# Seven half products for one more gate-side group of a fused S5 and SwiGLU block, placed beside an output pair

## The chip, the cores and the metric

The kernel runs on one core of one Trainium2 chip. The metric is device time in microseconds (us): 201.05 us is the median of three timed runs of the kernel before (200.91, 201.05 and 201.06). TensorE (PE in the profile) multiplies matrices, VectorE (DVE) and ScalarE (ACT) work elementwise, GpSimd (POOL) here mostly issues accumulating transfers, and SyncE (SP) issues loads and stores. Each engine takes its own instructions in the order in which the program gives them, and waits for the others by semaphores.

## The reference, cut to what matters

```python
xn = layernorm(x)                                # x: 1 x 2048 x 512, bf16
Bu = einsum("bld,pd->blp", xn, B_bar)            # complex, 512 states
h_t = Lam_bar * h_(t-1) + Bu_t                   # over 2048 tokens
y  = 2 * real(einsum("blp,dp->bld", h, C)) + xn * Dskip
glu = (silu(xn @ w1) * (xn @ w3)) @ w2           # 512 -> 1792 -> 512
out = x + y + glu
```

## The kernel before, in words

The 2048 tokens are worked in four blocks of 512 (`b` = 0 to 3). In a block the normalised input lies transposed in `xnT` (four tiles of 128 input features by 512 tokens). `glu` makes 14 tiles of 128 hidden features: gate side `xn @ w1` through Silu into a tile `g16`, up side `xn @ w3` into `u16`, and VectorE multiplies the two into `act`. `bu` makes the inputs of the scan. `ssm_tasks` holds VectorE's share of the state part: `pre_a`, `pre_b` and `pre_c` rotate `Bu` (`pre_c`, L491 to L495, is the last add of the rotation, on VectorE or as an accumulating transfer from GpSimd's queue), four scans per half of the states (L505), and `post_a`, `post_b`, `post_c` rotate the states back into `act`.

The outputs are made in eight pairs of 128-token chunks, `pairs[n]` with n = 0 to 7; pairs 4 and 5 belong to block 2, pairs 6 and 7 to block 3. `y_fast(n)` makes one pair by seven half products (Winograd's form of Strassen's method) of 11 matmuls each, called `product1` to `product7`, in the order 1, 4, 2, 6, 5, 7, 3; for n = 4 and 5 product 3 is put off into the next pair. VectorE prepares each pair with three row sums (`row_sums`, L992 to L1008, two or three on VectorE, the rest as a transfer) and a fourth, `s4` (L1091 to L1096). `seeds(n)` copies residual values into PSUM (the banks that TensorE writes) before the pair's products add to them.

The same seven-product form is used for the up side of block 3 in `glu_last`. The up side's first 12 tiles are three groups of four (`NG` = 3, n = 0 to 2). A group's seven products are here called one, five, two, six, seven, three and last, in the order in which they run. Each is four matmuls with 256 moving columns (`product`, L866 to L872). Product five needs the weight sum `s1`, six needs `s2`, seven `s3`, and three needs `s4`. `up_sums` (L826 to L836) makes `s1` to `s3` for all three groups on VectorE ahead of `glu_last`; `s4` is made per group (L909, L910). ScalarE copies partial results between PSUM banks (L857), and VectorE adds the shared sum `s5` to two results per group (L879). The gate side of all tiles is plain: `gate_side` (L859, `side` at L845 to L851) is four matmuls with 512 moving columns per tile. In each group the four gate tiles stand between the products. `gate` (L862 to L864) multiplies gate and up.

The order of VectorE's work is set by `Filler` (`bg`, L23 to L60). Background work is a queue of tasks with costs; `fill` records tasks while a running estimate of VectorE's time is not more than a lead of 1.7 us past a running estimate of TensorE's. `own` counts work that TensorE's results need at once. `flush(key)` records everything in the queue up to the last task with that key, whatever stands before it.

At the end of the program (L1238 to L1252) pair 3 is followed by `glu_last(3)`, and that by pairs 4 to 7.

Of the kernel before, what the change touches and what calls it, by code (L numbers as in the profile page):

```python
# [17 lines left out]
P = 128  # L18
# [45 lines left out]
def kernel(  # L64
# [397 lines left out]
    def ssm_tasks(b, posts_last=False, between=(), middle=(), late=()):  # L462
# [5 lines left out]
        def half(hf):  # L468
            psl = slice(2 * hf, 2 * hf + 2)
            st = {}  # L470

            def pre_a():
                if b == 0:
                    sin_step((2 * hf + 1, 1))
                    nc.vector.tensor_scalar(out=tabe[:, psl, 2, :], in0=tabe[:, psl, 1, :], scalar1=-1.0,
                                            scalar2=None, op0=ALU.mult)
                st["g"] = u_blk[b, hf]
                if (b, hf) == (3, 0):
                    st["p"] = up.tile(FULL, BF16, name="u")
                elif b == NBLK - 1:  # L480
                    st["p"] = xtp.tile([P, NDT, TBLK], BF16, name="xnT").rearrange("p (j r) t -> p j r t", r=2)
                else:
                    st["p"] = ssmw.tile(FULL, BF16, name="p")
                nc.vector.tensor_tensor(out=st["p"][:, :, ::-1, :], in0=st["g"], in1=tabe[:, psl, 2:0:-1, :],
                                        op=ALU.mult)

            def pre_b():
                nc.vector.tensor_tensor(out=st["g"], in0=st["g"], in1=tabe[:, psl, 0:1, :].to_broadcast(FULL),  # L488
                                        op=ALU.mult)

            def pre_c():  # L491
                if b == 0 or (b, hf) == (2, 0):
                    nc.vector.tensor_tensor(out=st["g"], in0=st["g"], in1=st["p"], op=ALU.add)
                else:
                    gp.dma_start(out=st["g"], in_=st["p"], accum_op=ALU.add)  # L495

            def scan(j, ri):
                pt = 2 * hf + j
                init = 0.0
                if b in (1, 2):  # L500
                    init = ends[:, hf, 2 * j + ri:2 * j + ri + 1]
                elif b > 2:
                    init = act_blk[b - 1][:, CPB - 1, k_state(pt, ri), P - 1:P]
                v = st["g"][:, j, ri, :]
                nc.vector.tensor_tensor_scan(out=v, data0=rho[:, pt:pt + 1].to_broadcast([P, TBLK]), data1=v,  # L505
                                             initial=init, op0=ALU.mult, op1=ALU.add)

            def post_a(csl=slice(0, CPB)):
                if "p16" not in st:
                    st["p16"] = ssmw.tile(FULL, BF16, name="p").bitcast(FP16).rearrange(  # L510
                        "p j r (c t) -> p (j r c t)", t=P).rearrange("p (c k t) -> p c k t", c=CPB, t=P)
                tsl = slice(csl.start * P, csl.stop * P)
                nc.vector.tensor_tensor(out=by_state(st["p16"][:, csl]), in0=by_chunk(st["g"][:, :, ::-1, tsl]),  # L513
                                        in1=by_chunk(tabe[:, psl, 2:0:-1, tsl]), op=ALU.mult)

            def post_b(csl=slice(0, CPB)):
                tsl = slice(csl.start * P, csl.stop * P)
                n = csl.stop - csl.start
                nc.vector.tensor_tensor(out=by_state(act_state(b, hf)[:, csl]), in0=by_chunk(st["g"][:, :, :, tsl]),  # L519
                                        in1=by_chunk(tabe[:, psl, 0:1, tsl]).to_broadcast([P, 2, 2, n, P]), op=ALU.mult)  # L520

            def post_c(csl=slice(0, CPB)):
                a, p16 = act_state(b, hf)[:, csl], st["p16"][:, csl]
                if b == NBLK - 1 and (hf == 1 or csl.start > 0):
                    nc.vector.tensor_tensor(out=a, in0=a, in1=p16, op=ALU.add)
                else:
                    gp.dma_start(out=a, in_=p16, accum_op=ALU.add)  # L527

            if (b, hf) == (1, 1):
                pre_c.ready = lambda: ("squares", 2, CPB - 1) in sins_done  # L530
            pre_a.ready = lambda: (b, hf) in u_blk
            scans = [lambda j=j, ri=ri: scan(j, ri) for j in range(2) for ri in range(2)]
            return (pre_a, pre_b, pre_c), scans, (post_a, post_b, post_c)

        (pre0, scans0, post0), (pre1, scans1, post1) = (half(hf) for hf in range(NPT // 2))

        transfers = (post0[2],) + (() if b == NBLK - 1 else (post1[2],)) + ((pre1[2],) if b > 0 else ()) + ((pre0[2],) if b in (1, 3) else ())

        def add(*fns):
            for fn in fns:  # L540
# [285 lines left out]
    def up_sums(b):  # L826
# [8 lines left out]
                for out, x, z, op in ((s1, a21, a22, ALU.add), (s3, a11, a21, ALU.subtract),  # L835
                                      (s2, s1, a11, ALU.subtract))]  # L836

    def glu_last(b):
        xnT = xnT_blk[b]
        s1, s2, s3, s4 = ups["s"]  # L840
# [33 lines left out]
        def halves(ps):  # L874
            return ps.rearrange("p (h t) -> p h t", h=2)

        def add(out, ps):
            bg.own(0.7)
            nc.vector.tensor_tensor(out=out, in0=halves(ps), in1=halves(s5), op=ALU.add)  # L879

        gates = []
        for f in range(4 * NG, NFT):
# [6 lines left out]
                gates.pop()()  # L889
            if f % 2 == 1:  # L890
                gates.append(lambda f=f, tiles=tiles: gate(f - 1, tiles))
        for n in range(NG):
            f0 = 4 * n
            a11, a12, a22, s1n, s2n, s3n, s4n = (v[:, :, n, :] for v in (
                up_quarter(0, 0), up_quarter(1, 0), up_quarter(1, 1), s1, s2, s3, s4))
            g, e = (ps_y.tile([P, TBLK], FP32, name="y_ps") for _ in range(2))
            f, z = (ps_bu.tile([P, TBLK], FP32, name="bu_ps") for _ in range(2))
            upper, lower = pair_tiles(), pair_tiles()
            product(g, a11, b11, True)
            copy(f, g)  # L900
            product(e, s1n, t1, True)
            copy(s5, e)
            gate_side(f0, upper[0])
            bg.fill(0.8)
            gates.pop()()
            product(f, a12, b21, False)
            product(g, s2n, t2, False)
            copy(e, g)
            bg.own(0.42)  # L909
            nc.vector.tensor_tensor(out=s4n, in0=a12, in1=s2n, op=ALU.subtract)  # L910
            copy(upper[1][:, :, 0:TH], halves(f))
            gate_side(f0 + 1, upper[0])
            bg.fill()
            product(g, s3n, t3, False)
            copy(z, g)
            add(lower[1][:, :, TH:TBLK], g)
            product(e, s4n, b22, False)
            add(upper[1][:, :, TH:TBLK], e)
            gate_side(f0 + 2, lower[0])
            bg.fill()  # L920
            gate(f0, upper)
            product(z, a22, t4, False)
            copy(lower[1][:, :, 0:TH], halves(z))
            gate_side(f0 + 3, lower[0])
            bg.fill()
            gates.append(lambda f0=f0, lower=lower: gate(f0 + 2, lower))
        seeds(4)
        return gates.pop()


    def res_list(b):
# [104 lines left out]
    def y_fast(n, then=(), between=()):  # L1036
# [50 lines left out]
        def product2():  # L1087
            if b == 0:
                bg.first(list(then))
            mms(f, v["a12"], weight(1, D1), False)  # L1090
            v["s4"] = v["a12"]  # L1091
            if n in (2, 3, 4, 5):
                gp.dma_start(out=v["s4"], in_=v["s2"], accum_op=ALU.add)
            else:
                bg.own(0.85, -1.1)
                nc.vector.tensor_tensor(out=v["s4"], in0=v["a12"], in1=v["s2"], op=ALU.add)  # L1096
            add(o1[:, D1], f, o1[:, D1])
            if last:
                store(c1, o1, D1)
            if n + 1 < len(pairs) and n not in (1, 2, 3) and n - 1 not in LATER:  # L1100
                seeds(n + 1)
            steps()

# [43 lines left out]
        for i in ((1, 5, 2, 6, 4, 3, 7) if b == 0 else (1, 2, 4, 6, 5, 7, 3) if b == 1 else ORDER.get(n, (1, 4, 2, 6, 5, 7, 3))):  # L1147
            if i == 3 and n in LATER:
                later[n] = product3
            else:  # L1150
                products[i - 1]()
            if i == 5 and n - 1 in later:
                later.pop(n - 1)()
                if n + 1 < len(pairs):
                    seeds(n + 1)
            if n in LATER:
                bg.fill()
            if between:
                for step in between.popleft():
                    step()  # L1160
                    bg.fill()
                if n == 3 and not between:
                    bg.first(up_sums(3))
            if n == 2 and i == 7:
                seeds(3)

    ln_alloc(0)
    ln1a, ln1b = ln_tasks_vector(1)
# [70 lines left out]
    y_done.append(2)  # L1239
    y_fast(3, (), bu_fast(3, 1))  # L1240
    bg.flush("up")
    gate = glu_last(3)
    gate()
    for n in range(4, len(pairs)):
        ahead = row_sums(n + 1, *pairs[n + 1]) if n + 1 < len(pairs) else ()
        if n > 4:
# [2 lines left out]
        if n == 5:  # L1249
            for t in (difference(3), *last_posts):  # L1250
                bg.add(*t)
        y_fast(n, ahead if n == 4 else ())  # L1252


# [28 lines left out]
```

## Time and profile before

| what | value |
|---|---|
| median of the timed runs | 201.05 us (200.91 to 201.06) |
| span of the profiled execution, first to last instruction | 199.5 us |
| TensorE busy | 195.6 us, 1401 matmuls |
| VectorE busy | 181.8 us, 254 instructions |
| ScalarE busy | 135.0 us, 281 instructions |
| GpSimd busy | 51.5 us, 75 instructions |
| mean granted TensorE clock | 0.999 |
| matmuls of `glu_last` | L848, 64 of them: 15.9 us; L869, 84 of them in groups of 24 and 12 |

No time of the profiled execution other than its span is listed beside the three timed runs. The 1.5 us between the span and the median lie around the first and the last instruction.

The profile page lists busy time per engine, the chain of work that ended last, groups of instructions by source line, and transfers. A timeline lists one engine's instructions in order: start and length in us, line, operation, tiles written and read, and in brackets the idle time just before it with what ended it. Consecutive instructions of one kind are merged (x2 is two). A matmul's listed length contains about 0.16 us of drain beyond its share of the pace, so the step from one start to the next is what it costs in a row. On VectorE too the next instruction often starts some 0.08 us before the listed end of the one before.

### The profile page before, as it was taken

Reading aid. Unit: us, or ns where it says so; the run is one execution under the profiler, and the core shown is the slowest. Engines: PE = TensorE matmul, PEld = TensorE weight load, DVE = VectorE, ACT = ScalarE, POOL = GpSimd, SP = SyncE. Lnnn points to the kernel's source line nnn. Section 1 sums busy time; section 2 is a strip of 40 time slices with the busy share of each in tenths; the row PEclk is TensorE's granted clock in tenths of the full one; section 3 lists DMA queues with packets and bytes.
Section 4 is the critical chain, followed back from the end, with each engine's and each line's share of the span. In section 5 each row is a group of like instructions: output and inputs, shape, how many; then the busy total and the mean of one; then the engine's idle time right before and its main releaser. Section 6 shows DMA issues by size and latency. Waiting matters only on the chain.

```text
span 199.5 us, 3700 instructions
## 1 busy us (share of the span) xinstructions
PE 195.6 (98%) x1401; PEld 130.7 (65%) x1401; DVE 181.8 (91%) x254; ACT 135.0 (68%) x281; POOL 51.5 (26%) x75
## 2 busy tenths in 40 slices
PE   8999999999999999999999999999999999999994
PEld 2774444444444488866555468888566678888893
DVE  3689699999999999989999997999999999999972
ACT  4699897699999996968998684362588783111220
POOL 7180289700411134041202305040021303310000
PEclk9999999999999999999999999999999999999999
DMA  4999996991497054730997455838137732941111
GB/s 138 326 277 200 302 186 124 343 273 23 69 181 141 0 105 82 135 105 0 156 148 119 89 92 98 172 83 132 53 59 129 149 56 52 174 92 36 53 44 40
DMA packets 32258, 25.12 MB, mean 126 GB/s; under 512 B 16240, under 2 KB 29936, under 8 KB 32240
## 3 DMA queue, kind: packets, MB, share of 16 engines
q0 software_dynamic: 6128, 11.38, 33.5%
q1 hardware_dynamic: 25536, 13.21, 26.8%
q10 hardware_dynamic: 576, 0.30, 0.5%
q8 instruction: 11, 0.18, 0.4%
q14 instruction: 7, 0.06, 0.1%
HBM read 7.74 MB, written 2.10 MB: 49 GB/s over the span
## 4 chain that ended last, share of the span: by engine, by line
PE 95%; DMA 2%; SPq 1%; issue 0%; DVE 0%
PE gu_ps L587 34%; PE gu_ps L1054 17%; PE y_ps L1054 10%; PE gu_ps L848 7%; PE bu_ps L1054 7%; PE bu_ps L454 3%; PE y_ps L454 3%; PE y_ps L869 3%; PE y_ps L780 3%; DMA w_sb<-in_B_w_dram 2%; PE gu_ps L619 2%; PE gu_ps L780 2%; PE bu_ps L869 1%; PE bu_ps L780 1%; PE bu_ps L619 1%; SPq L166 0%
## 5 line engine op out<-in xcount | busy, mean ns | idle before, releaser
L587 PE MATMUL gu_ps<-xnT,w_sb 128*128 128x512 bf16 x312 | 69.6, 379 | 0.0
L587 PEld LDWEIGHTS <-w_sb 128*128 128x128 bf16 x312 | 30.5, 98 | 34.2
L1054 PEld LDWEIGHTS <-act 128*128 128x128 f16 x462 | 43.5, 98 | 5.4
L596 ACT ACTIVATE g<-gu_ps 128x512 bf16<-128x512 f32 x41 | 24.8, 606 | 6.0 <-PE gu_ps L587 3.6
L597 ACT ACTIVATE u<-gu_ps 128x512 bf16<-128x512 f32 x41 | 24.8, 606 | 4.5 <-PE gu_ps L587 3.7
L505 DVE TENSOR_TENSOR_SCAN u<-rho,ends,u 128x512 bf16<-128x512 f32 x16 | 20.0, 1270 | 0.0
L527 POOL DMA_DIRECT2D act<-p x7 | 9.2, 1320 | 34.0 <-DVE act L519 22.1
L1054 PE MATMUL gu_ps<-w_sb,act 128*128 128x256 bf16 (+3 forms) x126 | 16.0, 267 | 0.0
L848 PE MATMUL gu_ps<-xnT,w_sb 128*128 128x512 bf16 x64 | 15.9, 379 | 0.0
L604 DVE TENSOR_TENSOR act<-g,u 128x1024 f16<-128x1024 bf16 x21 | 14.2, 679 | 0.4 <-ACT u L597 0.4
L860 ACT ACTIVATE g<-gu_ps 128x512 bf16<-128x512 f32 x14 | 8.4, 599 | 5.4 <-PE gu_ps L848 5.0
L454 PEld LDWEIGHTS <-bt 128*128 128x128 bf16 x64 | 6.3, 98 | 7.5
L1077 ACT ACTIVATE x_blk<-gu_ps 128x256 f32<-128x256 f32 (+1 forms) x9 | 3.3, 368 | 10.6 <-PE gu_ps L1054 10.6
L1054 PE MATMUL bu_ps<-w_sb,act 128*128 128x256 bf16 (+3 forms) x84 | 10.4, 264 | 0.0
L1054 PE MATMUL gu_ps<-ct,act 128*128 128x256 f16 (+1 forms) x72 | 10.4, 267 | 0.0
L848 PEld LDWEIGHTS <-w_sb 128*128 128x128 bf16 x64 | 6.3, 98 | 4.8
L505 DVE TENSOR_TENSOR_SCAN u<-rho,u 128x512 bf16<-128x512 f32 x8 | 9.2, 1206 | 0.0
L1054 PEld LDWEIGHTS <-x_blk 128*128 128x128 f16 x88 | 8.6, 98 | 1.0
L1054 PEld LDWEIGHTS <-tw 128*128 128x128 f16 x88 | 8.6, 98 | 1.0
L513 DVE TENSOR_TENSOR p<-u,tabe 128x2048 f16<-128x2048 bf16 (+1 forms) x8 | 8.7, 1085 | 0.1
L519 DVE TENSOR_TENSOR act<-u,tabe 128x2048 f16<-128x2048 bf16 (+1 forms) x8 | 8.7, 1083 | 0.0
L488 DVE TENSOR_TENSOR u<-u,tabe 128x2048 bf16<-128x2048 bf16 x7 | 8.5, 1219 | 0.1
(203 smaller groups left out, 392.5 us busy)
## 6 DMA issues: line engine op xcount, KB each, us to landing
act<-p POOLq DMA_DIRECT2D x6, 512.0 KB, 6.1
xn<-x_blk POOLq DMA_DIRECT2D x4, 512.0 KB, 5.5
out_dram<-xn SPq DMA_DIRECT2D x15, 128.0 KB, 1.7
w_sb<-in_B_w_dram SPq DMA_DIRECT2D x1, 1792.0 KB, 8.2
act<-act POOLq DMA_DIRECT2D x5, 352.0 KB, 4.6
w_sb<-in_B_w_dram SPq DMA_DIRECT2D x2, 768.0 KB, 6.4
u<-p POOLq DMA_DIRECT2D x3, 512.0 KB, 5.1
w_sb<-in_B_w_dram SPq DMA_DIRECT2D x4, 256.0 KB, 4.9
```

The source lines that it names most:

```text
L454: nc.tensor.matmul(out=ps, lhsT=bt[:, ri, dt, pt * P:(pt + 1) * P], rhs=xnT_blk[b][:, dt, :], start=(dt == 0), stop=(dt == NDT - 1))
L505: nc.vector.tensor_tensor_scan(out=v, data0=rho[:, pt:pt + 1].to_broadcast([P, TBLK]), data1=v, initial=init, op0=ALU.mult, op1=ALU.add)
L513: nc.vector.tensor_tensor(out=by_state(st["p16"][:, csl]), in0=by_chunk(st["g"][:, :, ::-1, tsl]), in1=by_chunk(tabe[:, psl, 2:0:-1, tsl]) ...
L519: nc.vector.tensor_tensor(out=by_state(act_state(b, hf)[:, csl]), in0=by_chunk(st["g"][:, :, :, tsl]), in1=by_chunk(tabe[:, psl, 0:1, tsl] ...
L527: gp.dma_start(out=a, in_=p16, accum_op=ALU.add)
L587: nc.tensor.matmul(out=ps[:, tsl], lhsT=w[:, dt, f * P:(f + 1) * P], rhs=xnT[:, dt, tsl], start=(dt == 0), stop=(dt == NDT - 1))
L596: nc.scalar.activation(out=g16[:, f % 2, :], in_=g_ps, func=ACT.Silu)
L597: nc.scalar.activation(out=u16[:, f % 2, :], in_=u_ps, func=ACT.Copy)
L604: nc.vector.tensor_tensor(out=act_gates(b, f - 1), in0=split(g16), in1=split(u16), op=ALU.mult)
L780: nc.tensor.matmul(out=out[:, h * TH:(h + 1) * TH], lhsT=left[:, h, k, :], rhs=right[:, k, :], start=(start and h == 0 and k == 0), stop=( ...
L848: nc.tensor.matmul(out=ps, lhsT=w[:, dt, f * P:(f + 1) * P], rhs=xnT[:, dt, :], start=(dt == 0), stop=(dt == NDT - 1))
L1054: nc.tensor.matmul(out=out, lhsT=left[:, k, :], rhs=right[k][:, cols], start=(start and k == 0), stop=(k == NK - 1), skip_group_check=True)
```

## The change

It has three parts.

1. The gate side of block 3's third group (n = 2) is made by seven half products too, in place of four tiles of plain matmuls. `gate_sums` makes their three weight sums with VectorE, each 128 x 512 elements; the tasks are added to the queue behind group 0 under the key "gs", and recorded by `bg.flush("gs")` at the first gate-side product. A fourth sum is made as for the up side. The two adds of `s5` write back to PSUM (`halves(ps)`), and ScalarE applies Silu from there; the other two results get Silu straight from PSUM.
2. The third group leaves `glu_last`. Its up products one and five and the outstanding `gate` run before pair 4; the other five up products and the seven gate products stand after the products 1, 4, 2, 6, 5 and 7 of pair 4, two or three at a time, with `fill` after each step. `seeds(5)`, which takes the same PSUM banks, moves from product 2 of pair 4 to the end of pair 4. The row sums stay as they were.
3. In block 2 the first half's `pre_c` becomes an accumulating transfer instead of a VectorE add.

```diff
@@ ssm_tasks
-                if b == 0 or (b, hf) == (2, 0):
+                if b == 0:
                     nc.vector.tensor_tensor(out=st["g"], in0=st["g"], in1=st["p"], op=ALU.add)
                 else:
                     gp.dma_start(out=st["g"], in_=st["p"], accum_op=ALU.add)
...
-        transfers = (post0[2],) + (() if b == NBLK - 1 else (post1[2],)) + ((pre1[2],) if b > 0 else ()) + ((pre0[2],) if b in (1, 3) else ())
+        transfers = (post0[2],) + (() if b == NBLK - 1 else (post1[2],)) + ((pre1[2],) if b > 0 else ()) + ((pre0[2],) if b > 0 else ())
@@ new
+    def gate_sums():
+        s1, s2 = (ups["s"][i][:, :, 0, :] for i in range(2))
+        a11, a12, a21, a22 = (gate_quarter(*i) for i in ((0, 0), (1, 0), (0, 1), (1, 1)))
+        s3, s4 = gate_quarter(0, 1, True), gate_quarter(1, 0, True)
+        ups["gs"] = a11, a12, a22, s1, s2, s3, s4
+        return [(0.42, lambda out=out, x=x, z=z, op=op: nc.vector.tensor_tensor(out=out, in0=x, in1=z, op=op), "gs")
+                for out, x, z, op in ((s1, a21, a22, ALU.add), (s3, a11, a21, ALU.subtract),
+                                      (s2, s1, a11, ALU.subtract))]
@@ glu_last: group() gives a group's seven products as steps; gated=True is the gate side
+            def add(out, ps):
+                bg.own(0.7)
+                nc.vector.tensor_tensor(out=halves(ps) if gated else out, in0=halves(ps), in1=halves(s5), op=ALU.add)
+                if gated:
+                    end(out, ps)
...
-        for n in range(NG):
+        for n in range(NG - 1):
...
+            if n == 0:
+                for t in gate_sums():
+                    bg.add(*t)
         seeds(4)
-        return gates.pop()
+        up_steps = group(lefts, lambda: sums4(lefts[6], lefts[1], lefts[4]), upper[1], lower[1], False)
+        state = {}
+        def gate_step(i):
+            def run():
+                if "steps" not in state:
+                    bg.flush("gs")
+                    right = ups["gs"]
+                    state["steps"] = group(right, lambda: sums4(right[6], right[1], right[4]), upper[0], lower[0], True)
+                state["steps"][i]()
+            return run
...
+        return (one, five, first), deque(((two, six), (seven, three), (last, gone, gfive), (gtwo, gsix),
+                                          (gseven, gthree), (glast, lambda: gate(f0, upper), lambda: gate(f0 + 2, lower))))
@@ y_fast
-            if n + 1 < len(pairs) and n not in (1, 2, 3) and n - 1 not in LATER:
+            if n + 1 < len(pairs) and n not in (1, 2, 3, 4) and n - 1 not in LATER:
                 seeds(n + 1)
...
-            if n == 2 and i == 7:
-                seeds(3)
+            if n in (2, 4) and i == 7:
+                seeds(n + 1)
@@ end of the program
-    gate = glu_last(3)
-    gate()
+    begin, beside = glu_last(3)
+    for step in begin:
+        step()
+        bg.fill()
...
-        y_fast(n, ahead if n == 4 else ())
+        y_fast(n, ahead if n == 4 else (), beside if n == 4 else ())
```

`gone`, `gfive`, `gtwo`, `gsix`, `gseven`, `gthree` and `glast` are the gate side's seven products.

More of the change, by code (lines that the diff above doesn't have):

```diff
@@ L836, in up_sums, with gate_quarter @@
                                       (s2, s1, a11, ALU.subtract))]
+    def gate_quarter(kh, r, half=False):
+        f0 = 4 * (NG - 1) * P
+        v = w1_sb[:, 2 * kh:2 * kh + 2, f0 + r * 2 * P:f0 + (r + 1) * 2 * P]
+        return v.bitcast(FP16) if half else v
+    def gate_sums():
[6 more added lines that the diff above has]
+                                      (s2, s1, a11, ALU.subtract))]
     def glu_last(b):
@@ L875, in halves, with group, end, one @@
             return ps.rearrange("p (h t) -> p h t", h=2)
-        def add(out, ps):
-            bg.own(0.7)
-            nc.vector.tensor_tensor(out=out, in0=halves(ps), in1=halves(s5), op=ALU.add)
+        def group(lefts, four, top, low, gated):
+            a11, a12, a22, s1n, s2n, s3n, s4n = lefts
+            g, e = (ps_y.tile([P, TBLK], FP32, name="y_ps") for _ in range(2))
+            f, z = (ps_bu.tile([P, TBLK], FP32, name="bu_ps") for _ in range(2))
+            def end(out, ps):
+                nc.scalar.activation(out=out, in_=halves(ps), func=ACT.Silu if gated else ACT.Copy)
+            def add(out, ps):
[3 more added lines that the diff above has]
+                    end(out, ps)
+            def one():
+                product(g, a11, b11, True)
+                copy(f, g)
+            def five():
+                product(e, s1n, t1, True)
+                copy(s5, e)
+            def two():
+                product(f, a12, b21, False)
+            def six():
+                product(g, s2n, t2, False)
+                copy(e, g)
+                four()
+                end(top[:, :, 0:TH], f)
+            def seven():
+                product(g, s3n, t3, False)
+                copy(z, g)
+                add(low[:, :, TH:TBLK], g)
+            def three():
+                product(e, s4n, b22, False)
+                add(top[:, :, TH:TBLK], e)
+            def last():
+                product(z, a22, t4, False)
+                end(low[:, :, 0:TH], z)
+            return one, five, two, six, seven, three, last
+        def sums4(out, x, z):
+            bg.own(0.42)
+            nc.vector.tensor_tensor(out=out, in0=x, in1=z, op=ALU.subtract)
+        def up_lefts(n):
+            return [v[:, :, n, :] for v in (up_quarter(0, 0), up_quarter(1, 0), up_quarter(1, 1), s1, s2, s3, s4)]
         gates = []
@@ L891, in glu_last @@
                 gates.append(lambda f=f, tiles=tiles: gate(f - 1, tiles))
-        for n in range(NG):
+        for n in range(NG - 1):
             f0 = 4 * n
[L894 to L897, printed above, removed]
+            lefts = up_lefts(n)
             upper, lower = pair_tiles(), pair_tiles()
[L899 to L902, printed above, removed]
+            one, five, two, six, seven, three, last = group(
+                lefts, lambda: sums4(lefts[6], lefts[1], lefts[4]), upper[1], lower[1], False)
+            one()
+            five()
             gate_side(f0, upper[0])
@@ L905, in glu_last @@
             gates.pop()()
[L906 to L911, printed above, removed]
+            two()
+            six()
             gate_side(f0 + 1, upper[0])
             bg.fill()
[L914 to L918, printed above, removed]
+            seven()
+            three()
             gate_side(f0 + 2, lower[0])
@@ L921, in glu_last @@
             gate(f0, upper)
-            product(z, a22, t4, False)
-            copy(lower[1][:, :, 0:TH], halves(z))
+            last()
             gate_side(f0 + 3, lower[0])
@@ L926, in glu_last @@
             gates.append(lambda f0=f0, lower=lower: gate(f0 + 2, lower))
+            if n == 0:
+                for t in gate_sums():
+                    bg.add(*t)
         seeds(4)
-        return gates.pop()
+        f0 = 4 * (NG - 1)
+        upper, lower = pair_tiles(), pair_tiles()
+        lefts = up_lefts(NG - 1)
+        up_steps = group(lefts, lambda: sums4(lefts[6], lefts[1], lefts[4]), upper[1], lower[1], False)
[8 more added lines that the diff above has]
+            return run
+        one, five, two, six, seven, three, last = up_steps
+        gone, gfive, gtwo, gsix, gseven, gthree, glast = (gate_step(i) for i in range(7))
+        first = gates.pop()
+        return (one, five, first), deque(((two, six), (seven, three), (last, gone, gfive), (gtwo, gsix),
+                                          (gseven, gthree), (glast, lambda: gate(f0, upper), lambda: gate(f0 + 2, lower))))
     def res_list(b):
```

## The prediction, made before the changed kernel ran

> **What bounds the kernel now.** I read the page's busy times first, then the chain of work that ended last.
>
> ```profile
> PE 195.6 (98%) x1401; PEld 130.7 (65%) x1401; DVE 181.8 (91%) x254; ACT 135.0 (68%) x281; POOL 51.5 (26%) x75
> ...
> PE 95%; DMA 2%; SPq 1%; issue 0%; DVE 0%
> ```
>
> TensorE is the bound: it holds 95% of the chain, and its timeline has no idle time from 7.16 us to its end at 196.8. So a matmul removed is worth its pace, and a new wait of TensorE costs its full length. VectorE, at 91%, is the engine from which a wait would come. Next I read both engines' timelines around the third group, TensorE's first.
>
> ```profile
> 156.40 0.60 PE L869 MATMUL y_ps<-xnT,w_sb 128*128 128x256 bf16 x4
> ...
> 157.27 1.03 PE L848 MATMUL gu_ps<-xnT,w_sb 128*128 128x512 bf16 x4
> 158.13 0.60 PE L869 MATMUL bu_ps<-xnT,w_sb 128*128 128x256 bf16 x4
> ```
>
> By the steps between starts a product is 0.436 us (157.27 less 156.40 is two of them) and a gate tile 0.864 (158.13 less 157.27). Eleven matmuls of a pair's product take 1.20 (170.14 to 171.34 in the same view).
>
> ```profile
> 156.03 0.88 DVE L1000 TENSOR_TENSOR x_blk<-act 128x1408 f16<-128x1408 f16 x1
> 156.83 0.68 DVE L864 TENSOR_TENSOR act<-g,u 128x1024 f16<-128x1024 bf16 x1
> 157.44 0.88 DVE L1000 TENSOR_TENSOR x_blk<-x_blk,act 128x1408 f16<-128x1408 f16 x1
> 158.24 0.68 DVE L864 TENSOR_TENSOR act<-g,u 128x1024 f16<-128x1024 bf16 x1
> 158.84 0.42 DVE L910 TENSOR_TENSOR w_sb<-w_sb,bt 128x512 f16<-128x512 bf16 x1
> 159.18 2.45 DVE L505 TENSOR_TENSOR_SCAN u<-rho,act,u 128x512 bf16<-128x512 f32 x2
> ...
> 171.02 3.63 DVE L505 TENSOR_TENSOR_SCAN x_blk<-rho,act,x_blk 128x512 bf16<-128x512 f32 x3
> ```
>
> VectorE is packed here: no brackets, one instruction on the next. The fourth sum of group 2 (L910) ends at 159.26, ahead of product three, which needs it and starts at 160.33. The scans, 1.2 us each, stand behind it.
>
> **TensorE's saving: 0.4 us.** Removed are four gate tiles, 4 x 0.864 = 3.46; added are seven products, 7 x 0.436 = 3.05. The other five up products only move. That is 0.2% of the run, just what a measurement of this kernel can tell from no change (about 0.2%).
>
> **First new wait: product three of the up side, 1.7 us.** The transfer in place of `pre_c` frees VectorE of 1.14 us (L493 starts at 107.73, the next instruction at 108.87), so later background work is recorded that much sooner. I walk VectorE's new queue from 148.29, where both programs wait for the same ScalarE copy. From there to the start of group 2's fourth sum the old queue took 158.84 - 148.29 = 10.55, 0.31 of it idle. The new one holds one rotation multiply fewer (1.13, now done earlier), no idle time, 0.1 more between two row sums that now follow each other, and all four scans of the first state half (4.8) ahead of this sum. It starts at 148.29 + 10.55 - 1.13 - 0.31 + 0.1 + 4.8 = 162.3 and ends at 162.7. TensorE starts the group at 156.40 as before and comes to product three after one, five, product 1, two, six, product 4 and seven: 156.40 + 5 x 0.436 + 2 x 1.20 = 160.98. It waits 1.7, with its whole queue behind it.
>
> **Second new wait: product five of the gate side, 9.7 us.** It needs the first "gs" sum. The flush of that key records all that the queue holds before it. In the changed program's order VectorE has, between the add that follows product 2 of pair 4 and this sum, two row sums, two rotation multiplies, the four scans of the second state half, two multiplies and an add. None of these needs TensorE, and the transfer that the scans need was issued some 15 us sooner (such transfers land in 4.6). By steps between starts: the add 0.34 (L1065), row sums 0.91 and 0.81 (L1000, 179.54 to 181.26), multiplies 0.60 and 0.60 (L513, L519, from 169.08), scans 4.9 (3.6 by the row above, and 175.48 to 176.79), multiplies 0.61 and 0.72, the add 0.60 (L525), the sum 0.42 (as L910): 10.5, and 0.1 of hand-overs. TensorE has only `last` and `gone` for this time, 0.87. The wait is 10.6 - 0.87 = 9.7. TensorE had no other waits that this could fill, so nothing is given back.
>
> **The clock after it: 1.8 us.** First a stretch of the windows view (last three columns: granted clock, transfers' share, GB/s), then TensorE's first row.
>
> ```profile
> 198.00:199.00 1.00, 0.00 (x0) 0.00 (x0) 0.00 (x0) 0.00 (x0) 0.00 (x0) 1.00 0.15 33
> 199.00:199.50 0.50, 0.00 (x0) 0.00 (x0) 0.00 (x0) 0.00 (x0) 0.00 (x0) 0.57 0.00 0
> ```
>
> ```profile
> 0.76 4.16 PE L196 MATMUL bu_ps<-const-bfloat16-1.0 128*128 128x512 bf16 x10 [0.76 <-PEq L1267]
> ```
>
> TensorE stops at 196.8, and some 2.3 us later its clock falls. A wait of 9.7 passes that, one of 1.7 doesn't. What it costs to come back I take from the start: ten matmuls took 4.16, less 0.16 of drain, where the later pace (16 in 3.46 from 139.88) gives 2.16. So 1.8 is lost. The bounds are none (the clock stays) and twice as much.
>
> [...]
>
> **Two smaller waits: 0.6 and 1.2 us.** Pair 5's first product reuses the PSUM bank of gate product seven. After seven come on ScalarE a copy (0.60), on VectorE two adds into PSUM (0.60 and 0.68, as L879) and on ScalarE the two Silus (0.6, then the second at 0.6 behind the second add): with hand-overs 0.63 + 0.63 + 0.68 + 0.63 = 2.6. TensorE has gthree, product 7 and glast meanwhile, 2.07. It waits 0.6; an add that writes back to PSUM isn't in the trace, and I take L879's row, which reads the same and writes elsewhere. Pair 7's first two products need the second token half's rotations, which the new order puts behind pair 6's last output add, because the estimate in `Filler` has VectorE far ahead. Add 0.38, the half's last add 0.68, against 0.77 of matmuls that don't need it, with hand-overs 0.43 of wait; then two multiplies and an add, another 0.8. Together 1.2; in the old order both were done in time (185.21 and 188.69).
>
> **What costs nothing.** ScalarE's four added copies replace no time on TensorE's path: 4 x 0.6 in a stretch where it is busy 4.62 of 15.5 us (163.0 to 178.5). The transfer for `pre_c` is issued near 108 and lands in about 5.1; its scan comes near 116. It moves GpSimd's queue: pair 3's fourth sum now starts behind a 512 KB transfer, 0.6 later (132.8). Alone it lands in 3.8, and behind another the slowest took 9.1, where product 3 wants it at 138.8: nothing to 1 us, most likely nothing.
>
> **Sum.** -0.4 + 1.7 + 9.7 + 1.8 + 0.6 + 1.2 = +14.6. On the profiled span: 199.5 + 14.6 = 214.1; the median stood 1.5 above the span: 215.6 us.
>
> **Rivals.**
> - *The clock stays up, or the small waits are absorbed.* With the clock up 215.6 - 1.8 = 213.8; without the small waits too, 212.0. For it: the drop is shown only at the program's end. Chance 0.12.
> - *A costlier return.* The slow spell lasts twice as long (+1.8) and pair 3 waits for its transfer (+1): 218.4. For it: spells may start anywhere. Chance 0.06.
> - *Faster, 200.65 us.* VectorE reaches the first "gs" sum before TensorE wants it at 165.2, so only the 0.4 counts. This needs 9.7 us less in front of that sum, and decides at product five: each us that VectorE is later than 165.2 costs one. Against it: the list above has no member that could be skipped. Chance 0.03.
> - *No change.* VectorE is late at product five by only 0.2 to 0.6 us, and the waits cancel the saving: 201 us. Against it the same list. Chance 0.01.
>
> Forecast 0.78. The range takes in the no-drop case less half the small waits, 213.0, and the doubled spell, 217.4 with 0.6 for the transfer, 218.0. Faster 0.03, same 0.01, slower 0.96.
>
> **What would show it.** In the changed profile: TensorE idle before L883 by about 1.7 and 9.7 us, ended by DVE w_sb (L939) and DVE bt (L848); two slices of TensorE far below 9 near 165 to 175, and a granted clock below 1 just after; an idle time before y_ps (pair 5) ended by ACT, and two before pair 7 ended by DVE L525. If the scans stand before the sums and TensorE still shows no idle time, the walk is wrong.

## The result, and the profile after

The changed kernel takes 217.82 us (median of five runs, 217.06 to 218.13) beside 201.06 us of the kernel before on the same chip: ratio 1.0818, 95% interval 1.0795 to 1.0841. The profiled execution took 217.08 us, its span is 214.9 us.

From the page after: busy times, the slices of TensorE and of its granted clock, and the chain of work that ended last.

```profile
PE 197.1 (92%) x1400; PEld 132.2 (62%) x1413; DVE 183.7 (85%) x259; ACT 137.0 (64%) x285; POOL 52.9 (25%) x76
...
PE   8999999999999999999999999999995039899984
...
PEclk9999999999999999999999999999999658999999
...
PE 19%; DVE 13%; DMA 3%; ACT 2%; issue 1%; ACTq 0%
```

The chain is followed back only to a transfer of pair 3 near 132 us, so its shares add up to 38% of the span and not to nearly all of it, as before. Of these 38, VectorE holds 13, where its share was 0% before. Of TensorE's slices one is empty and the two beside it hold half and a third of their length in work; the granted clock is low in the empty one and in the two behind it (6, 5 and 8 tenths). The waits of TensorE say which work ended each of them (columns: total us, times, longest):

```profile
PE y_ps L883 <- DVE bt L848: 9.7, 1, 9.7
PE y_ps L883 <- DVE w_sb L939: 1.6, 1, 1.6
PE y_ps L1130 <- DVE act L525: 0.9, 2, 0.6
...
PE y_ps L1130 <- ACT g L897: 0.6, 1, 0.6
PE bu_ps L1130 <- DMA act<-tw: 0.4, 1, 0.4
```

What VectorE does in the long wait, from its timeline after:

```profile
165.32 0.88 DVE L1076 TENSOR_TENSOR tw<-act 128x1408 f16<-128x1408 f16 x1
166.24 0.89 DVE L1076 TENSOR_TENSOR tw<-tw,act 128x1408 f16<-128x1408 f16 x1
167.04 0.68 DVE L513 TENSOR_TENSOR p<-u,tabe 128x1024 f16<-128x1024 bf16 x1
167.65 0.68 DVE L519 TENSOR_TENSOR act<-u,tabe 128x1024 f16<-128x1024 bf16 x1
168.25 4.80 DVE L505 TENSOR_TENSOR_SCAN x_blk<-rho,act,x_blk 128x512 bf16<-128x512 f32 x4
173.09 0.69 DVE L513 TENSOR_TENSOR p<-x_blk,tabe 128x1024 f16<-128x1024 bf16 x1
173.69 0.69 DVE L519 TENSOR_TENSOR act<-x_blk,tabe 128x1024 f16<-128x1024 bf16 x1
174.41 0.69 DVE L525 TENSOR_TENSOR act<-act,p 128x1024 f16<-128x1024 f16 x1
175.02 0.42 DVE L848 TENSOR_TENSOR bt<-w_sb 128x512 f16<-128x512 bf16 x1
```

The list has no brackets: VectorE works throughout, and the sum that TensorE waits for (L848) is the last line. TensorE over the same time, from its timeline after:

```profile
165.21 0.60 PE L883 MATMUL y_ps<-xnT,w_sb 128*128 128x256 bf16 x4
175.50 1.04 PE L883 MATMUL y_ps<-x_blk,bt 128*128 128x256 f16 x4 [9.68 <-DVE bt L848]
176.32 2.56 PE L1130 MATMUL gu_ps<-tw,x_blk 128*128 128x256 f16 x11
178.67 0.73 PE L883 MATMUL bu_ps<-xnT,w_sb 128*128 128x256 bf16 x4
179.24 0.60 PE L883 MATMUL y_ps<-x_blk,bt 128*128 128x256 f16 x4
```

Eleven matmuls take 2.56 us here, 1.36 elsewhere: half clock (0.50 granted). The windows of the same stretch (granted clock is the third column from the end) give its end:

```profile
168.90:175.50 6.60, 0.00 (x1) 0.01 (x1) 6.50 (x9) 0.00 (x0) 0.93 (x1) 0.50 0.53 85
175.50:178.90 3.40, 3.40 (x17) 2.40 (x18) 0.73 (x2) 0.60 (x1) 0.00 (x0) 0.50 0.02 5
178.90:181.00 2.10, 2.10 (x21) 1.88 (x20) 0.85 (x2) 1.06 (x2) 0.00 (x0) 0.99 0.00 0
```

### The profile page after: what moved, and what is told of

Same layout as the page of the kernel before. It is cut to its first block, busy times and chain, and to the rows that moved or that the text cites. A ratio compares the mean times of both kernels' runs of the same rounds, so it can differ in the third digit from the quotient of the medians.

```text
span 214.9 us, 3727 instructions
## 1 busy us (share of the span) xinstructions
PE 197.1 (92%) x1400; PEld 132.2 (62%) x1413; DVE 183.7 (85%) x259; ACT 137.0 (64%) x285; POOL 52.9 (25%) x76
## 5 line engine op out<-in xcount | busy, mean ns | idle before, releaser
L587 PE MATMUL gu_ps<-xnT,w_sb 128*128 128x512 bf16 x304 | 68.9, 379 | 0.4
L587 PEld LDWEIGHTS <-w_sb 128*128 128x128 bf16 x312 | 30.5, 98 | 34.2
L596 ACT ACTIVATE g<-gu_ps 128x512 bf16<-128x512 f32 x41 | 24.8, 606 | 6.0 <-PE gu_ps L587 3.1
L883 PE MATMUL y_ps<-x_blk,bt 128*128 128x256 f16 x32 | 5.2, 290 | 9.7 <-DVE bt L848 9.7
L862 PE MATMUL gu_ps<-xnT,w_sb 128*128 128x512 bf16 x45 | 11.5, 379 | 0.1
L883 PEld LDWEIGHTS <-w_sb 128*128 128x128 bf16 (+1 forms) x80 | 7.9, 99 | 4.9 <-DVE w_sb L939 1.9
L1130 PEld LDWEIGHTS <-x_blk 128*128 128x128 f16 x88 | 9.2, 104 | 1.6
L883 PEld LDWEIGHTS <-bt 128*128 128x128 f16 x32 | 3.2, 102 | 10.4 <-DVE bt L848 10.0
L1130 PE MATMUL gu_ps<-tw,x_blk 128*128 128x256 f16 x66 | 9.4, 297 | 0.0
L874 ACT ACTIVATE g<-gu_ps 128x512 bf16<-128x512 f32 x10 | 6.0, 599 | 5.1 <-PE gu_ps L862 4.4
```

Of the source, the lines that this page charges most:

```text
L587: nc.tensor.matmul(out=ps[:, tsl], lhsT=w[:, dt, f * P:(f + 1) * P], rhs=xnT[:, dt, tsl], start=(dt == 0), stop=(dt == NDT - 1))
L596: nc.scalar.activation(out=g16[:, f % 2, :], in_=g_ps, func=ACT.Silu)
L862: nc.tensor.matmul(out=ps, lhsT=w[:, dt, f * P:(f + 1) * P], rhs=xnT[:, dt, :], start=(dt == 0), stop=(dt == NDT - 1))
L874: nc.scalar.activation(out=g16[:, f % 2, :], in_=side(w1_sb, f), func=ACT.Silu)
L883: nc.tensor.matmul(out=out[:, h * TH:(h + 1) * TH], lhsT=left[:, k, h * P:(h + 1) * P], rhs=right[:, k, :], start=(start and h == 0 and k ...
L1130: nc.tensor.matmul(out=out, lhsT=left[:, k, :], rhs=right[k][:, cols], start=(start and k == 0), stop=(k == NK - 1), skip_group_check=True)
```

## The experiments

The theory at the start was that of the prediction: VectorE's *order* makes the waits. The rival was the *amount* of VectorE's work: three weight sums, a fourth and two adds are 2.6 us more (4 x 0.34 + 2 x 0.62), the transfer gives back 1.1, and an engine at 91% cannot take the rest.

### The gate sums recorded early

```diff
             if n == 0:
-                for t in gate_sums():
-                    bg.add(*t)
+                bg.first(gate_sums())
```

> The three "gs" sums go to the front of VectorE's background queue at the end of group 0, and the key's flush then finds nothing to record. Theory (the flush puts 10 us of scans and rotations ahead of a sum that TensorE waits for): the wait of 9.7 us before product five of the gate side and the 1.7 us of slow clock behind it go, the waits before product three, pair 5 and pair 7 stay in part or move, the one on pair 3's transfer (0.5) stays: 202 to 205 us. Rival (VectorE simply has too much to do beside pair 4, wherever the sums stand): TensorE waits nearly as long at the next thing that it needs from VectorE, and the time stays above 212 us.

Measured: 209.57 us (208.37 to 211.87), ratio 1.0414 (1.0381 to 1.0447). The 9.7 us and the half clock behind it are gone from the profile, whose mean granted clock is 1.0 and whose span is 207.2. But both expectations missed. The first wait grew from 1.6 to 2.87 us, and new waits came up in pair 6 (1.33, ended by L525) and pair 7 (1.08 and 0.56). The sums stand in front, so the rest stands later. The first wait in VectorE's timeline:

```profile
159.45 4.80 DVE L505 TENSOR_TENSOR_SCAN u<-rho,act,u 128x512 bf16<-128x512 f32 x4
164.17 0.40 DVE L939 TENSOR_TENSOR w_sb<-w_sb,bt 128x512 f16<-128x512 bf16 x1
```

Four scans without a gap ahead of group 2's fourth sum. What puts them there is a second flush, of the key ("scan", 3), which `y_fast(4)` makes as it starts. It stood behind the third group before, and stands ahead of its fourth sum now.

### The same, with the rotation's last add back on VectorE

```diff
-                if b == 0:
+                if b == 0 or (b, hf) == (2, 0):
```

> As e1_front, with the last add of block 2's first rotation back on VectorE. Theory: pair 3's wait of 0.4 to 0.6 us for its transfer goes, since GpSimd's queue is as before; VectorE is 1.1 us later, so at most one scan fewer stands ahead of product three's sum: between 1.2 us faster than e1_front and 0.5 slower. Rival (the transfer buys VectorE time that TensorE gets): 1 us or more slower than e1_front.

Measured: 216.07 us (213.6 to 217.47), ratio 1.0741 (1.0716 to 1.0766): 6.5 us more than with the transfer. The theory allowed at most 0.5 us more; it fell, and the rival held: the transfer buys VectorE time that TensorE gets. 1.14 us of VectorE's work reach TensorE's first wait (2.87 becomes 4.01) and, with the row sums and rotations behind them, the later ones (2.23 and 1.68). Three times the waits also halve the clock in the profiled execution (granted 0.50 from 164 to 170 us and from 192 to 194, 0.56 from 206 to 208). It is the slowest of the seven (217.47 us, mean clock 0.967; of the others five have 0.976 and one 0.992), so its waits are shown, but not that each run lost the clock as often. The last section returns to that. One part of the theory held: pair 3's wait for its transfer is gone.

### The transfer alone

The kernel before with only part 3 of the change.

> The kernel before with the third part of the change alone, the rotation's last add by transfer. Theory: VectorE's relief is worth nothing where TensorE never waits, and the order of GpSimd's queue costs pair 3's product 3 a wait of 0.4 to 0.6 us: 201.3 to 201.7. Rival (the transfer is free, pair 3's wait came from something else): 201.0 to 201.1.

Measured: 201.59 us (201.18 to 202.06), ratio 1.0031 (1.0017 to 1.0045). One new wait, in TensorE's timeline of this run:

```profile
139.26 0.94 PE L1054 MATMUL bu_ps<-w_sb,act 128*128 128x256 bf16 x7 [0.40 <-DMA act<-tw]
```

Pair 3's fourth sum stands behind the 512 KB transfer in GpSimd's queue. By itself the transfer costs 0.55 us by the medians, as the theory had it; what it frees on VectorE brings nothing as long as VectorE isn't late.

### TensorE kept busy in the long wait

The changed kernel with 42 matmuls of 512 columns on a constant, into a bank that is overwritten, ahead of product five of the gate side. They add nothing to the outputs.

```diff
             def five():
+                if gated:
+                    for _ in range(42):
+                        nc.tensor.matmul(out=e, lhsT=ones[:, 0:P], rhs=ones[:, 0:TBLK], start=True, stop=True)
                 product(e, s1n, t1, True)
```

> The changed kernel with 42 matmuls of 512 columns on constant ones ahead of product five of the gate side, into the PSUM bank that this product overwrites: 42 x 0.216 = 9.1 us of work inside a wait of 9.7. Theory (the wait halves the clock for 3.4 us of work): TensorE runs at full clock after it, 1.5 to 1.9 us faster than the changed kernel, 215.9 to 216.4. Rival (the clock is not what the extra time beyond the waits is): 217.5 to 218.

Measured: 215.21 us (214.95 to 215.53), ratio 1.0707 (1.0682 to 1.0732): 2.6 us less than the changed kernel by the medians, 1.9 less by the spans of the profiled executions (213.0 and 214.9). The gain is larger than the expected 1.5 to 1.9; the point on the clock, further down, takes it apart. TensorE's timeline:

```profile
165.41 9.35 PE L912 MATMUL y_ps<-const-bfloat16-1.0 128*128 128x512 bf16 x42
175.26 0.61 PE L883 MATMUL y_ps<-x_blk,bt 128*128 128x256 f16 x4 [0.50 <-DVE bt L848]
175.71 1.36 PE L1133 MATMUL gu_ps<-tw,x_blk 128*128 128x256 f16 x11
```

Counted from the first matmul of `glu_last`, product five starts as late as in the changed kernel (35.2 us behind it in both), but the products behind it run at full pace (1.36 in place of 2.56; granted clock 1.00 from 173 to 178 us). So the clock is a cost of its own, on top of the wait.

### The scans behind the fourth sum

On top of the early gate sums.

```diff
-        if p == 0 and b > 1:
+        if p == 0 and b > 1 and n != 4:
             bg.flush(("scan", b + 1))
...
+                if n == 4 and at == 5:
+                    bg.flush(("scan", 3))
+                    bg.first(list(then))
```

The second piece stands behind product three (`at` counts the steps left beside pair 4). The row sums for pair 5 (`then`) also come there, since they overwrite what the scans start from, and the `fill` calls after the group's steps are left out up to that point.

> On top of the version with the gate sums recorded early: the four scans of the first state half, which pair 4 records as it starts, and the row sums for pair 5 behind them, now come after group 2's fourth sum. Theory (the order on VectorE makes the waits): the 2.87 us before the product that needs that sum goes; left are 0.6 to 0.9 before pair 5, 0.4 before pair 3's product 3, and some 3.3 in pairs 6 and 7: 205 to 206.5 us. Rival (the amount of VectorE's work makes them: sums and adds for the gate side are 2.6 us more, the transfer gives back 1.1): the 2.9 us turn up again before pairs 6 and 7, 209 to 210 us.

Measured: 205.49 us (205.28 to 205.92), ratio 1.022 (1.0203 to 1.0237). The 2.87 us are gone and did not turn up elsewhere: pair 6 still waits 1.33, pair 7 1.08 and 0.56, as in the version with the early sums, and pair 5 0.71. Against the rival.

### Only the gate side's own sums taken out of the queue

The changed kernel, but the three "gs" tasks are moved to the front before the flush.

```diff
                 if "steps" not in state:
+                    own = [t for t in bg.tasks if t[2] == "gs"]
+                    bg.tasks = deque(t for t in bg.tasks if t[2] != "gs")
+                    bg.first(own)
                     bg.flush("gs")
```

> The changed kernel, but where the gate side's first product needs its sums, only these three are taken out of the queue; what stands before them stays queued. Theory (the 9.7 us is what the flush drags in): this wait and the half clock behind it go, the 1.6 us before it stays, 0.6 before pair 5, 0.4 at pair 3, and 3 to 3.5 us come up in pairs 6 and 7 for the work that is recorded later: 206.5 to 208.5 us. Rival (VectorE is simply that far behind at this place, whatever the order): a wait of over 5 us stays before product five of the gate side, over 212 us.

Measured: 207.9 us (207.66 to 208.27), ratio 1.0341 (1.0322 to 1.036). TensorE's waits:

```profile
PE y_ps L1133 <- DVE act L525: 1.6, 2, 1.1
PE y_ps L883 <- DVE w_sb L939: 1.6, 1, 1.6
PE gu_ps L1133 <- DVE act L525: 1.3, 1, 1.3
...
PE y_ps L1133 <- ACT g L897: 0.6, 1, 0.6
PE bu_ps L1133 <- DMA act<-tw: 0.4, 1, 0.4
```

This is the cleanest of the tests: three lines, at the same place, take 9.9 us off the changed kernel by the medians and 9.2 by the spans of the profiled executions (214.9 and 205.7). VectorE was not behind at this place; the flush made it so. The 1.6 us stay, and waits ended by L525 add up to 2.9 us in place of 0.9.

### Longer leads, then other PSUM banks

On top of the scans behind the fourth sum: first, `fill` in pairs 5 and 6 records up to 3.5 us ahead, and block 2's first 512 KB transfer is put behind two more scans.

```diff
+    LEADS = {5: 3.5, 6: 3.5}
-            bg.fill()
+            bg.fill(LEADS.get(n))
...
-            add(*post0, *scans1, *post1)
+            if b == 2:
+                add(*post0[:2], *scans1[:2], post0[2], *scans1[2:], *post1)
+            else:
+                add(*post0, *scans1, *post1)
```

> The version of the scans behind the fourth sum, and two changes more: in pairs 5 and 6 background work is recorded up to 3.5 us ahead of TensorE instead of 1.7 (1.2 at one place), and block 2's first 512 KB transfer is put two scans later, behind pair 3's own. Theory (order): the waits of pairs 6 and 7 and the one of pair 3 go, 0.6 to 0.9 before pair 5 stays, and the saving of 0.4 is had: span 199.5 + 0.2 to 0.5, 201.2 to 202.3 us with what lies outside the span in these versions. Rival (amount of work): VectorE can't be further ahead, waits of 2 us and more stay in pairs 6 and 7: 203.5 us or more.

Measured: 201.49 us (201.34 to 201.87), ratio 1.0019 (1.001 to 1.0029). One wait is left, 0.71 us before pair 5, ended by ScalarE's Silu (L900): the waits of pairs 6 and 7 and that of pair 3 are gone, against the rival. These are two edits in one run, so it doesn't show by itself which of them removed which wait. Then the wait that is left:

```diff
+        if n == 5:
+            f = ps_bu.tile([P, TBLK], FP32, name="bu_ps")
+            e = ps_bu.tile([P, TBLK], FP32, name="bu_ps")
+            g = ps_gu.tile([P, TBLK], FP32, name="gu_ps")
+            z = early.pop()
```

`early` holds a bank of `ps_gu` that is seeded ahead of the gate side's products seven and three; pair 6 takes two banks of `ps_y` in exchange, and the leads are 3 us.

> As the version with the longer leads (3 us), and pair 5's first product and one of its seeds use PSUM banks that pair 4 has left, instead of the gate side's, so that they don't stand behind the two Silus; pair 6 takes two banks of the other kind in exchange. Theory (order): the 0.6 to 0.9 before pair 5 goes; VectorE is then the next to be late, by 0 to 0.6 at pair 6: 200.7 to 202.0 us. If all of it went, the saving of 0.4 would show as 200.65. Rival (amount of work): 203.5 us or more, as without the banks.

Measured: 201.34 us (200.99 to 201.59), ratio 1.0013 (1.0003 to 1.0023). One wait again, 0.38 us before pair 6's product 4, ended by L525.

### Late output adds, and the transfer once more

```diff
         bg.flush(("sums", n))
+        while delayed:
+            delayed.pop()()
...
             mms(g, v["s3"], tsum[2], False)
+            if n in (5, 6):
+                delayed.append(end7)
+            else:
+                end7()
```

`end7` is product 7's add with its store, unchanged.

> As the version with the other banks, and the last output add of pairs 5 and 6 (0.6 us of VectorE each) is recorded behind the next pair's row sums, with leads of 4 and 3 us. Theory (order, and no slack left on VectorE): the 0.38 before pair 6's product 4 goes, at most 0.2 comes up in pair 7: span 199.1 to 199.4, 200.8 to 201.2 us; without any wait the saving of 0.4 would stand whole, 200.65. Rival (amount of work: VectorE is full, what is taken from one place turns up at the next): 201.2 to 201.6 us as before this edit.

Measured: 200.74 us (200.38 to 201.21) beside 200.94 of the kernel before on the same chip: ratio 0.9989, 95% interval 0.9979 to 0.9998. All waits of TensorE that the profile lists:

```profile
PE bu_ps L196 <- PEq L1385: 0.8, 1, 0.8
PE y_ps L243 <- DVE xn L224: 0.2, 1, 0.2
```

Both lie in the first 5 us of the program. So the seven gate products, at the place that the change gives them, cost nothing once VectorE's order and the banks are right, and the version is 0.2 us faster than the kernel before: half of the 0.4 that the counts promise, and at the edge of what can be told apart. The expected range (200.8 to 201.2, span 199.1 to 199.4) was missed by a little, on the fast side: the profiled span is 198.6, and pair 7 shows no wait.

The same version with the rotation's last add back on VectorE:

> As the version with the late output adds, but the rotation's last add of block 2's first half is back on VectorE (1.14 us) instead of a transfer. Theory (VectorE has no slack from there to pair 6, so its 1.14 us reach TensorE, and the row sums behind come late too): waits of about 1.2, 0.5 and 0.5 in pairs 6 and 7, 202.3 to 203.4 us. Rival (once the order is right VectorE has slack, and the transfer is not needed): as with the transfer, within 0.4 us.

Measured: 203.13 us (202.79 to 203.54), ratio 1.0116 (1.0101 to 1.0132).

```profile
PE y_ps L1156 <- DVE act L525: 1.4, 2, 0.9
...
PE y_ps L1156 <- DVE q L1167: 0.3, 1, 0.3
```

As expected, and against its rival: here the amount does count. With the order right VectorE is just in time up to pair 6; 1.14 us more of work there cost 2.4.

## Why the prediction was right, point by point

The time came out 2.2 us above the forecast and inside the range. It is nearer to the rival of the costlier return (218.4) than to the forecast (215.6), but not by that rival's main term.

The prediction took each wait as the time by which TensorE's next start is put off, beyond the pace. The list of waits shows less: it counts from the listed end of the matmul before, which holds some 0.16 us of drain beyond the pace. So the points below give both, the listed wait and the cost by steps between starts.

- **Product three of the up side, 1.7 us:** listed 1.59; by steps 1.75 (160.94 to 163.13, less 0.44). The scans stand ahead of the sum as walked. The walk had the order right; that a flush of its own sets it was seen only when the scans stayed there with the gate sums in front.
- **Product five of the gate side, 9.7 us:** listed 9.68; by steps 9.85 (165.21 to 175.50, less 0.44). The flush is shown as its cause by taking only the own sums out. What the prediction did not say is that recording this work early is worth something later: without the flush 2.0 us come back in waits ended by L525. The flush's net cost, clock included, is 9.2 by the spans and 9.9 by the medians.
- **The clock, 1.8 us:** by the rows 1.7, since 3.43 us of work ran at half clock. Keeping TensorE busy gained 1.64 from the first matmul of `glu_last` to the start of the last group of four (71.48 us in the changed kernel, 69.84 with the constant's matmuls), which agrees. The other 0.25 of the 1.9 between the spans lies ahead of `glu_last`, where the edit changes nothing, and the rest of the 2.6 is that the changed kernel's median run was 0.7 longer than its profiled one. That the size fits is in part luck. The prediction had the clock fall 2.3 us after TensorE stops, and priced the return from the program's start, where ten matmuls take 0.40 us each against 0.216 later; but the windows of the kernel before show a granted clock of 1.00 there, from 0 to 5 us, so the trace doesn't show that a low clock makes the start slow. Here it fell 2.9 us after (165.8 to 168.69), and behind the 4.01 us wait of the version with the add on VectorE 4.97 us of work ran at half clock (165.27 to 170.24), which is 2.5 us lost. So neither the 2.3 nor the 1.8 is a fixed figure.
- **The smaller waits, 0.6 and 1.2 us:** before pair 5 listed 0.62, by steps 0.78. The prediction's own two numbers, 2.6 and 2.07, give 0.5, so this wait was taken too small. In pair 7 listed 0.35 and 0.55, by steps 0.52 and 0.71, together the 1.2 of the sum.
- **What "costs nothing":** this step failed for pair 3's transfer. "Nothing to 1 us, most likely nothing" was 0.40 of listed wait and 0.56 by steps, in the changed kernel and alone. The prediction leaned on the 3.8 us in which this transfer lands when alone; behind the 512 KB it took 6.6 (issued at 132.45, product 3 starts at 139.06).
- **The saving, 0.4 us:** had in the matmuls, not quite in the time. In the version without waits the first matmul of `glu_last` to the start of the last group of four takes 56.28 us (139.20 to 195.48), before 56.51 (139.88 to 196.39): 0.23. The rest goes in steps of pair 6 that are too little late for the list: 1.29 in place of 1.20 (178.64 to 179.93), 0.51 in place of 0.44 (180.70 to 181.21) and 1.22 in place of 1.20 right behind.
- **Sum and what lies around the span:** by steps the terms are 1.75 + 9.85 + 1.7 + 0.78 + 1.23 + 0.56 - 0.4 = 15.5 where the prediction had 14.6. On the span before, 199.5, that gives 215.0; the profiled span is 214.9. So these terms account for the whole of it, and of the 0.8 by which the span passes the predicted 214.1 most is pair 3's transfer. The other 1.4 us of the miss is in two places. The times stand 2.2 us above the spans of their runs, where the prediction took 1.5; that was the median of some executions less the span of another, and runs of the kernel before on these chips stand 1.8 above their own spans. And the span of the median run was 215.6, 0.7 above the profiled one. What lies behind either is open.

Of the rivals, "faster" named the right point: it asked for a VectorE that reaches the gate sums in time, and by the experiments this wait was a matter of three lines and not of VectorE's load. Its 200.65 us took more than that: with the three lines alone the time was 207.9, and 200.74 needed the other edits of order, leads and banks too. The prediction held against it that no member of VectorE's list could be skipped. That holds for the list as recorded; but none had to be skipped, they only had to stand behind the sums.

## What to carry to other kernels

A flush by key records everything that stands ahead of the key. Before steps are moved past a flush, or tasks are put at the end of a queue for a consumer that comes soon, list what the flush will drag in and compare it with the bounding engine's work until then. And when an engine at 90% turns late after a change, test its order before its load: here one order cost 17 us and another, with other PSUM banks, nothing, with the same instructions on VectorE. But its load is not free either: 1.14 us more of it cost 2.4 with the order right, and 6.5 with only the gate sums in front.

## What the runs showed of the clock

A wait need not be long to halve TensorE's clock. In the profile of the version with the early sums and the add on VectorE, the clock fell in the wait of 4.01 us, after the one of 2.23, and after those of 1.68 and 0.55 together. The windows around the second (granted clock third from the end; the wait ends at 190.39):

```profile
190.00:192.00 2.00, 1.61 (x9) 1.22 (x10) 1.97 (x4) 0.38 (x1) 0.00 (x0) 0.68 0.00 0
192.00:194.00 2.00, 2.00 (x12) 1.44 (x10) 1.66 (x4) 0.00 (x0) 0.00 (x0) 0.50 0.00 0
194.00:196.00 2.00, 2.00 (x20) 1.74 (x19) 1.19 (x3) 0.00 (x0) 0.00 (x0) 0.97 0.00 0
```

A mean of 0.68 in the first window, with 1.00 in the two us before it and 0.50 in the window behind, means half clock for 1.28 of its 2 us, so the clock fell at 190.72, after TensorE was back at work. Worked out in this way the clock was low in that profile from 163.4 to 170.2, from 190.7 to 194.1 and from 204.4 to 207.8 us, and in the changed kernel's from 168.69 to 178.93. In the long waits it fell 2.1 and 2.9 us after TensorE had stopped (161.3 to 163.4, 165.8 to 168.69).

The length of a single wait doesn't tell whether the clock falls. It fell after 2.23 us, and after 1.68 and 0.55 with 1.4 us of work between them. The changed kernel's first wait, 1.59, kept it (1.00 from 160 to 165 us), and so did the longer wait of 2.87 in the version with the early sums, in the profiled execution (1.00 from 161.7 to 167 us; mean clock 1.0, span 207.2). Two other runs of that kernel show a mean clock of 0.992 with a span of 208.4; without a trace of them it isn't shown which wait lost it there. What decides, beside the length of the wait, these runs don't show.
